# Loads of the FFN weights issued behind the DMA that turns the negated cosines

## The chip, the cores and the metric

The kernel runs on one core of a Trainium2 chip. The metric is the device time of one execution in microseconds (us). Every run also gives its span, from the first instruction to the last, which is some 1.8 us shorter than the time. Unless said otherwise, runs are fast (a run more than 1.5% above the fastest of its kernel is marked slow), and times in a profile count from the start of its span.

## The reference

A pre-LN block on x of 2048 x 512: a spectral filter, then an FFN with squared ReLU, both with residuals.

```python
X = rfft2(layernorm(x)) * (w_r + 1j * w_i)
h = x + irfft2(X)
r = relu(layernorm(h) @ w1 + b1)         # 512 -> 1792
out = h + (r * r) @ w2 + b2              # 1792 -> 512
```

## The kernel before

The two FFTs are matmuls against tables of sines and cosines that the kernel makes itself. Stage 4 (the first inverse step) needs tables in the other orientation, the tile EI, with four parts: sine, cosine, negated sine, negated cosine. Each is a DMA transpose ("turn") from SBUF to SBUF, issued on the queue of SyncE (SP), which issues all plain loads too. The part that the change touches, with the pieces of work that come after it in program order:

```python
def turned(dst, src):
    nc.sync.dma_start_transpose(out=dst, in_=...)

table_c(slice(1, 8))                                  # ScalarE: cosines
turned(EI[:, 1:8, 1, :], EF[:, 1, 1:8, :])            # the turn of the cosines
def cos_negs():                                       # runs at "cn.0" of ORDER
    nc.vector.tensor_scalar(Cn[:], EF[:, 1, 1:8, :], -1.0, None, ALU.mult)
    turned(EI[:, 1:8, 3, :], Cn[:])                   # EI<-Cn, the turn in question
# ... (first pieces of stage 2)
for k, (dst, src) in enumerate(((W1[:], ...), (W2[:], ...), (b1b[:], ...), (b2b[:], ...))):
    load = nc.sync.dma_start(dst, src)                # 1792 KB, 1792 KB, 3.5 KB, 128 KB
    ...
def to_sqrt():                                        # "sq.0"
    nc.gpsimd.tensor_copy(b1f[:], b1b[:])
    nc.scalar.activation(junk1[:], eps[:], ACT.Sqrt, bias=eps[:])   # loads the table of Sqrt
ORDER = """ gn.0 s3.0 ... xa.0 cn.0 ...               # s4.k: matmuls of stage 4, slice k
    ... t.4 x.7 t.3 sq.0 s4.5 s4.6 A.7 B.7 y.7 z.7 m.7 n.7 t.5 t.6 s4.7 v.7 t.7 """
```

"x" and "t" are copies out of PSUM, the memory that matmuls write to (t.k into the tile T2 that stage 5 reads), mostly on ScalarE; v.7 is VectorE's half of the last. Most slices of stage 4 use sums and differences M of their data ("alternating halves of Z and M"). Only slices 5 and 6 work on Z itself, and they alone read the fourth part of EI:

```python
NO_M = (5, 6)
if M is None:                                         # slices 5 and 6; the line L500 of the profile
    en = ei[:, 2 * P:4 * P]                           # negated sine and negated cosine
    mms = [(u, r, ei[:, P:3 * P]) for u in range(2)]
    mms += [(u, 1 - r, en if u == r else ei[:, 0:2 * P]) for u in range(2)]
    for k, (u, c, tb) in enumerate(mms):
        nc.tensor.matmul(o, lhsT=Z[:, u, c, e::2], rhs=tb, start=(k == 0), stop=(k == 3))
```

## Time and profile before

| what | value |
|---|---|
| time, three runs | 164.94 us median (164.76 to 164.95) |
| the execution that was profiled | 164.48 us, span 162.7 us |
| negated cosines ready / EI<-Cn issued / landed | 22.7 / 37.5 / 41.7 us |
| stage-4 matmuls that read it could start | 40.9 us |
| first use of W1, of b1, of b2 | 53.0, 53.7, 61.7 us |

The time and the profiled execution are not of the same run, and they differ by 0.46 us. How busy the DMA engines are is seen by stretches of time. The columns are: stretch and its length, busy time (and instructions) of TensorE, its weight loads, VectorE, ScalarE and GpSimd, TensorE's granted clock (as a share of full speed), mean busy share of the 16 DMA engines, GB/s.

```profile
30.00:35.00 5.00, 4.95 (x42) 3.91 (x41) 5.00 (x13) 4.44 (x5) 0.00 (x0) 1.00 1.05 379
38.50:41.70 3.20, 2.53 (x21) 1.93 (x20) 3.17 (x8) 2.62 (x4) 0.27 (x1) 1.00 0.88 102
41.70:45.50 3.80, 3.73 (x35) 3.34 (x35) 2.79 (x7) 3.29 (x5) 0.00 (x0) 1.00 0.00 0
```

The engines are full while W comes in, the last stretch before 41.7 holds the end of the loads of b1 and b2 and then the turn, in small pieces (1003 of 1091 packets are under 512 bytes) at about a quarter of the rate, and afterwards there is no traffic. TensorE has 0.67 us unused in the middle row.

### The profile page before, as it was taken

What the parts mean: (1) busy time and instruction counts of PE and PEld (TensorE: products, weight loads), DVE (VectorE), ACT (ScalarE), POOL (GpSimd) and SP (SyncE); (2) the same over time, 40 slices, a digit from 0 to 9 for tenths busy, and PEclk for the clock granted to TensorE, in tenths of its full rate; (3) what the DMA queues carried; (4) which work ended last, traced back from release to release, by engine and by line L of the source; (5) the groups of instructions that cost most, each with busy time, mean ns of one, the idle gap of its engine ahead of it and who ended that gap; (6) DMA issues with size and microseconds to landing.
All of it is one profiled execution on the core that took longest, in us unless ns stands there. A gap on an engine that the chain in (4) does not pass through costs nothing.

```text
span 162.7 us, 2708 instructions
## 1 busy us (share of the span) xinstructions
PE 149.7 (92%) x934; PEld 87.5 (54%) x947; DVE 124.8 (77%) x320; ACT 105.5 (65%) x203; POOL 36.7 (23%) x64
## 2 busy tenths in 40 slices
PE   3959899999887999999899999999999999999990
PEld 1537675877663874666345454434454444565470
DVE  6999899999847798699995588995379984377221
ACT  4989889898967780598552897731389760288000
POOL 7868840000000005025000235000052300052000
PEclk9999999999999999999999999999999999999999
DMA  5986299999100000200000100024300005210011
GB/s 157 344 263 127 64 189 220 395 358 123 25 0 0 4 0 2 66 5 0 0 32 32 36 0 0 2 65 103 94 0 2 0 0 129 65 36 0 4 61 34
DMA packets 16430, 12.34 MB, mean 76 GB/s; under 512 B 10784, under 2 KB 14880, under 8 KB 16416
## 3 DMA queue, kind: packets, MB, share of 16 engines
q1 hardware_dynamic: 16256, 11.25, 25.8%
q0 software_dynamic: 160, 0.92, 2.6%
q8 instruction: 7, 0.11, 0.3%
q14 instruction: 7, 0.06, 0.1%
HBM read 8.01 MB, written 2.10 MB: 62 GB/s over the span
## 4 chain that ended last, share of the span: by engine, by line
PE 62%; DVE 22%; ACT 5%; issue 3%; DMA 3%; POOL 3%; ACTq 0%; DVEq 0%; POOLq 0%
PE po L742 26%; PE ph L709 21%; DVE act L713 4%; DVE st L217 3%; DMA EI<-Cn 3%; PE p L500 2%; PE po L730 2%; ACT rl L712 2%; PE p L346 2%; PE p L606 1%; POOL rs L224 1%; DVE Z L463 1%; DVE mB L456 1%; DVE mA L456 1%; DVE hs L610 1%
## 5 line engine op out<-in xcount | busy, mean ns | idle before, releaser
L712 ACT ACTIVATE rl<-ph,b1f 128x384 bf16<-128x384 f32 (+2 forms) x70 | 41.2, 616 | 22.4 <-PE ph L709 20.7
L709 PE MATMUL ph<-UT,W 128*128 128x384 bf16 (+2 forms) x277 | 51.5, 336 | 0.8 <-DVE UT L820 0.6
L742 PE MATMUL po<-W,act 128*128 128x512 bf16 x204 | 46.8, 379 | 0.3
L716 POOL TENSOR_TENSOR hb<-hs,b2b 128x512 f32<-128x512 bf16 x16 | 18.6, 1166 | 88.6 <-DVE act L713 88.6
L713 DVE TENSOR_TENSOR act<-rl 128x384 bf16<-128x384 bf16 (+2 forms) x70 | 31.3, 483 | 9.3 <-ACT rl L712 9.1
L709 PEld LDWEIGHTS <-W 128*128 128x128 bf16 x280 | 26.9, 98 | 21.1 <-issue 1.3
L742 PEld LDWEIGHTS <-act 128*128 128x128 bf16 x210 | 20.3, 98 | 24.8 <-issue 1.7
L746 DVE TENSOR_TENSOR ot<-po,hb 128x512 bf16<-128x512 f32 x15 | 10.3, 688 | 12.5 <-PE po L742 11.1
L257 PE MATMUL p<-ones 128*128 128x512 bf16 x22 | 7.1, 461 | 2.9 <-POOL ones L153 2.8
L243 PE MATMUL p<-KFr,xs 128*128 128x256 bf16 x32 | 7.3, 272 | 2.2 <-DVE KFr L228 2.2
L610 DVE SCALAR_TENSOR_TENSOR hs<-p,xs 128x512 bf16<-128x512 f32 x14 | 9.1, 681 | 0.0
L585 ACT CAST V<-p 128x512 bf16<-128x512 f32 x14 | 8.1, 593 | 0.0
L217 DVE BATCH_NORM_STATS2 st<-xs 128x6 f32<-128x512 bf16 x12 | 7.9, 677 | 0.0
L508 ACT CAST T<-p 128x1024 bf16<-128x1024 f32 x7 | 7.2, 1032 | 0.5 <-PE p L500 0.5
L245 PE MATMUL p<-KFr,xs 128*128 128x256 bf16 x32 | 7.3, 272 | 0.0
L346 PE MATMUL p<-GF,Bt 128*128 128x256 bf16 x56 | 7.1, 273 | 0.0
L621 ACT ACTIVATE junk<-hs 128x512 bf16<-128x512 bf16 x6 | 3.8, 628 | 5.1 <-DVE hs L610 5.1
L463 DVE TENSOR_TENSOR Z<-mA,mB 128x512 bf16<-128x512 bf16 x16 | 6.3, 422 | 0.6 <-PE p L500 0.5
L257 PEld LDWEIGHTS <-ones 128*128 128x128 bf16 x32 | 3.4, 110 | 6.2 <-POOL ones L153 2.8
L346 PEld LDWEIGHTS <-Bt 128*128 128x128 bf16 x56 | 5.5, 98 | 1.3
L383 ACT CAST U<-p 128x1024 bf16<-128x1024 f32 x6 | 6.1, 1032 | 0.0
L636 ACT ACTIVATE sd<-mv,eps 128x1 f32<-128x1 f32 (+2 forms) x10 | 2.7, 294 | 5.1 <-DVE mv L625 5.0
(188 smaller groups left out, 226.3 us busy)
## 6 DMA issues: line engine op xcount, KB each, us to landing
W<-in_B_w_dram SPq DMA_DIRECT2D x2, 1792.0 KB, 10.0
out_dram<-ot SPq DMA_DIRECT2D x15, 128.0 KB, 1.8
xs<-in_A_x_dram SPq DMA_DIRECT2D x3, 512.0 KB, 6.5
WB<-in_A_w_r_dram SPq DMA_DIRECT2D x1, 578.2 KB, 6.5
WB<-in_A_w_i_dram SPq DMA_DIRECT2D x1, 578.2 KB, 7.6
xs<-in_A_x_dram SPq DMA_DIRECT2D x2, 256.0 KB, 3.1
b2b<-in_B_b_dram SPq DMA_DIRECT2D x1, 128.0 KB, 9.4
out_dram<-ot SPq DMA_DIRECT2D x2, 64.0 KB, 1.5
```

The source lines that it names most:

```text
L217: nc.vector.bn_stats(st[:], xs[:, g, :])
L257: nc.tensor.matmul(o, lhsT=ones[:, 0:P], rhs=ones[:], start=True, stop=True)
L346: nc.tensor.matmul(puv[:, :, e, :], lhsT=Bt[:, 2 * t + 1 - e, 2 * pr + q, :], rhs=GFv[:, t, :, e, :], start=(t == 0), stop=(t == 1))
L463: nc.vector.tensor_tensor(Zs[pr][:, :, h], mA[:, :, h], mB[:, :, 1 - h], ALU.add if h else ALU.subtract)
L585: nc.scalar.copy(V[:].rearrange("p e h c -> p (e h c)"), pe[:])
L610: nc.vector.scalar_tensor_tensor(hs[:, g, :], Ys.pop(g)[:], WSC, xs[:, g, :], ALU.mult, ALU.add)
L709: nc.tensor.matmul(ph[:, 0:n], lhsT=W1[:, d, bass.ts(f, P)], rhs=UT[:, d, 0:n], start=(d == 0), stop=(d == ND - 1))
L712: nc.scalar.activation(rl[:, 0:n], ph[:, 0:n], ACT.Relu, bias=b1f[:, f:f + 1], scale=1.0)
L713: sq = nc.vector.tensor_tensor(act[:, f, 0:n], rl[:, 0:n], rl[:, 0:n], ALU.mult)
L716: add = nc.gpsimd.tensor_tensor(hb[:, g, :], hs[:, g, :], b2b[:], ALU.add)
L742: nc.tensor.matmul(po[:], lhsT=act[:, f, bass.ts(i, P)], rhs=W2[:, f, :], start=(f == 0), stop=(f == NF - 1))
L746: nc.vector.tensor_tensor(ot[:], po[:], hb[:, g, :], ALU.add)
```

## The change

Its intent is to send the turn that is wanted at 40.9 us ahead of the loads that are wanted from 53 us on. The loads become a function called just after the turn has been issued; nothing else changes.

```diff
-    for k, (dst, src) in enumerate(((W1[:], ...), (W2[:], ...), (b1b[:], ...), (b2b[:], ...))):
-        load = nc.sync.dma_start(dst, src)
-        ...
+    def first_loads():
+        cos_negs()
+        loads()
+
+    def loads():
+        for k, (dst, src) in enumerate(((W1[:], ...), (W2[:], ...), (b1b[:], ...), (b2b[:], ...))):
+            load = nc.sync.dma_start(dst, src)
+            ...
-                  ... cn=lambda k: cos_negs())
+                  ... cn=lambda k: first_loads())
```

More of the change, by code (lines that the diff above doesn't have):

```diff
@@ L515 @@
     stage2_one(1, 1, nc.scalar.copy)
-    for k, (dst, src) in enumerate(((W1[:], B_w1.rearrange("(c p) f -> p c f", p=P)),
-                                    (W2[:], B_w2.rearrange("(i p) d -> p i d", p=P)),
-                                    (b1b[:], B_b1.rearrange("(i p) -> p i", p=P)),
-                                    (b2b[:], B_b2.unsqueeze(0).to_broadcast([P, D])))):
-        load = nc.sync.dma_start(dst, src)
-        if k == 0:
-            for ga in gathers:
-                after(load, ga, "the rows of W first")
+    def first_loads():
+        cos_negs()
+        loads()
+    def loads():
+        for k, (dst, src) in enumerate(((W1[:], B_w1.rearrange("(c p) f -> p c f", p=P)),
+                                        (W2[:], B_w2.rearrange("(i p) d -> p i d", p=P)),
+                                        (b1b[:], B_b1.rearrange("(i p) -> p i", p=P)),
+                                        (b2b[:], B_b2.unsqueeze(0).to_broadcast([P, D])))):
+            load = nc.sync.dma_start(dst, src)
+            if k == 0:
+                for ga in gathers:
+                    after(load, ga, "the rows of W first")
     def angle_tables(k):
@@ L539 @@
                   s4=lambda k: stage4(k, split=(k == 7)), t=t_copy, v=t_copy, gi=lambda k: angle_tables(0),
-                  gn=lambda k: angle_tables(1), sq=lambda k: to_sqrt(), cn=lambda k: cos_negs())
+                  gn=lambda k: angle_tables(1), sq=lambda k: to_sqrt(), cn=lambda k: first_loads())
     ORDER = """
```

## The prediction

> **What bounds the kernel now.** I read the page first: the chain that ended last, for the line that has to do with the change. Most of it is TensorE in the FFN (L742 and L709); one entry belongs to the moved DMA.
>
> ```profile
> PE 62%; DVE 22%; ACT 5%; issue 3%; DMA 3%; POOL 3%; ACTq 0%; DVEq 0%; POOLq 0%
> ```
>
> So the DMA that turns the negated cosines (EI<-Cn) lies on the path that sets the end. Next the same chain in order of time (start, duration, what), around that DMA:
>
> ```profile
> 37.48 4.24 DMA EI<-Cn
> 41.77 3.45 PE p L500 x30
> 45.24 0.70 ACT T L508
> 46.17 0.58 ACT T L508
> 46.79 0.61 PE p L770 x4
> ```
>
> The chain walks from the landing of the DMA (41.72) to the stage-4 matmuls of L500, to the two ScalarE copies into T, to the first matmuls of stage 5. The 4.24 us are not what the DMA costs, since all engines had other work until 40.87. What it costs is read from the waits between 40 and 48 us (in total, times, longest):
>
> ```profile
> PE p L500 <- DMA EI<-Cn: 0.7, 1, 0.7
> DVE Z L463 <- PE p L500: 0.5, 1, 0.5
> ACT T L508 <- PE p L500: 0.5, 1, 0.5
> ```
>
> One wait of TensorE for the landing, and two that follow from it: VectorE wants a Z buffer that the late matmuls still read, ScalarE wants their result. Why does the DMA start at 37.48? The rows of the tile Cn say that its input was ready 15 us sooner, at 22.2 + 0.46 = 22.7:
>
> ```profile
> L332 DVE TENSOR_SCALAR Cn<-EF x1: 456/456/456, 22.2 to 22.2; 128x896 bf16<-128x896 bf16 x1
> ```
>
> The timeline of the queue SP says what it stood behind (start, time the queue was held):
>
> ```profile
> 19.16 5.90 SPq L260 DMA_TRANSPOSE EI<-EF  x4
> 25.48 0.94 SPq L520 DMA_DIRECT2D W<-in_B_w_dram  x2
> 26.47 5.03 SPq L520 DMA_DIRECT2D b1b<-in_B_b_dram  x1
> 31.55 5.83 SPq L520 DMA_DIRECT2D b2b<-in_B_b_dram  x1
> 37.48 2.20 SPq L260 DMA_TRANSPOSE EI<-Cn  x1
> ```
>
> Four loads hold the queue from 25.48 to 37.38, and none is wanted soon: W is first read at 53.0 (rows of the tile W), b1 by the activations from 53.71, b2 by GpSimd from 61.7. Last, ScalarE's timeline from 40 to 47 us, with the idle time before an instruction in brackets:
>
> ```profile
> 40.32 1.01 ACT L432 CAST X<-p 128x1024 bf16<-128x1024 f32 x1 [0.58 <-ACT T L508]
> 41.23 1.02 ACT L508 CAST T<-p 128x1024 bf16<-128x1024 f32 x1
> 42.27 1.28 ACT L533 ACT_TABLE_LOAD   x1
> 43.56 0.29 ACT L533 ACTIVATE junk<-eps 128x1 f32<-128x1 f32 x1
> 43.76 0.99 ACT L508 CAST T<-p 128x1024 bf16<-128x1024 f32 x1
> 45.24 1.01 ACT L508 CAST T<-p 128x1024 bf16<-128x1024 f32 x1 [0.48 <-PE p L500]
> 46.15 0.59 ACT L508 CAST T<-p4a 128x512 bf16<-128x512 f32 x1
> ```
>
> This engine is occupied without a break from 40.32 to 44.76 whatever the DMA does; only its 0.48 us before 45.24 come from the late matmuls. That row decides the size of the gain.
>
> **What the Trainium skill says.** The page "DMA: Bandwidth & Descriptors", section "Queues, rings and completion order": descriptors of one issuing queue are consumed in ring order on each DMA engine. So a transfer issued behind 3.6 MB of loads also moves behind them. The trace agrees: EI<-Cn lands at 41.72, after b2b's 31.55 + 9.4 = 40.95. "Perfetto Trace Analysis", section "Summary: the profiler window per engine type", says that a queue's row shows the issue and not the movement of data; here 2.20 us against 4.24 to the landing. The first page's "Rules for kernel authors" says that a non-contiguous last dimension becomes one descriptor per element; b1b, 3.5 KB in 2-byte pieces, holds the queue 5.03 us where each 1.8 MB load of W takes some 0.45. "ScalarE: Activation LUTs", section "What ACT_TABLE_LOAD costs", has about 1283 ns for the table load; the row above has 1.28 us.
>
> **The change part by part.** No instruction is added or removed, and the order on TensorE, VectorE, ScalarE and GpSimd stays; the listing of both kernels shows only SP changed: EI<-Cn goes from behind the four loads to ahead of them.
>
> (a) EI<-Cn. It becomes ready to issue when the queue is done with the previous turns, 19.16 + 5.90 = 25.06, Cn being there since 22.7. The turn just before it, of the same 7 blocks, held the queue 1.25 us and landed after 3.1 us. Taking 3.1 to 4.2 us, EI<-Cn lands at about 28.5 to 29.5, some 11 us before its first reader at 40.87. The DMA wait disappears.
>
> (b) The loads. They start later by what the turn takes in the queue and in the engines, 1.3 to 2.2 us: W1 lands near 35 instead of 25.48 + 7.4 = 32.9, W2 near 40 instead of 38.5, b1b and b2b near 42 to 43 instead of 41. From 20 to 37 us the DMA engines are busy 100% of the time and after 41.7 there is no traffic, so the same bytes in another order should end at about the same time. The margin to 53.0 is over 9 us. Cost on the path: none.
>
> (c) TensorE. The two first matmuls of L500 run at 40.65 as before; the other 30 start at 40.87 instead of 41.77, which frees 0.90 us (0.73 of it shown as idle, the rest modelled tail). At 0.109 us each, the 14 left of slice 5 end at 42.4; slice 6 needs Z, ready at 41.76, and ends at 44.15. Slice 7 takes 0.87, to 45.0 instead of 45.9.
>
> (d) VectorE. Its Z of slice 7 started at 43.49 with 0.53 idle. It is now free at 42.9, after slice 5 has been read (42.6), so M ends at 44.45 instead of 45.05; slice 7 reads the second half of M at 44.15 + 0.44 = 44.6. No new wait.
>
> (e) ScalarE. Slice 5's copy starts at 43.76 as before, because table load and X copy precede it. Slice 6's, whose matmuls are now done at 44.3, starts as soon as ScalarE is free: 45.24 - 0.48 = 44.76 (or 43.76 + 0.91 = 44.67, by the spacing of 45.24 to 46.15). The last copy starts at 45.6 to 45.7 instead of 46.15, its matmuls being done at 45.1.
>
> (f) Stage 5 at L770 waits for that copy: 46.79 - 0.5 = 46.3. From there every link is an engine waiting for an engine, so the tail shifts as a block.
>
> Sum: of the 0.90 us freed on TensorE about 0.5 come through, since ScalarE, not the DMA, is then the last to arrive. 164.94 - 0.5 = 164.4 us; span 162.7 to about 162.2.
>
> **The rivals.** First, the whole 0.9 us comes through (164.0). For it: the X copy at 40.32 has 0.58 us idle ahead of it, put down to a copy that ended at 39.74, so its real cause is unknown; VectorE, TensorE, or a stall that has to do with the busy DMA engines then. If the reordering removes it, ScalarE starts its last run up to 0.4 earlier, and TensorE's 0.9 is the limit. Against: nothing in the wait names a DMA.
>
> Second, the gain is eaten earlier (164.8 to 165.2). The turn now runs at 25 to 29 beside turns and gathers, where stage 3 feeds the chain through ScalarE; copies of one shape took 1.05 to 1.08 between 36 and 39 us and 1.01 to 1.04 otherwise. Ten copies slower by 0.05 would cost half a microsecond. Against: in that stretch VectorE is the busier engine, and ScalarE has a few tenths spare.
>
> Third, the loads become the wait: W or the biases arrive after 53 us and FFN matmuls stall (166 or more). It would need a delay of over 9 us where I see 2. Very unlikely.
>
> Fourth, nothing moves because another wait takes the place of this one at 40.87 (164.9): slice 6 needs a PSUM buffer, but the copy that frees it ended at 39.74. Unlikely.
>
> **Range and chances.** The runs of before lie within 0.2 us, so the spread is that of the rivals: 163.9 if the first holds fully, about 165.0 if the second eats the gain. I take 163.9 to 165.0 for 8 in 10, with 164.4 as the prediction. A change of 2% would be 3.3 us, beyond what any wait in the profile allows: 1% faster, 98% within, 1% slower.
>
> **What would show it.** Right: in the SP timeline EI<-Cn near 25.1 and W behind it; no wait of L500 for EI<-Cn; L500 as one run of matmuls from about 40.65; no idle ahead of ScalarE's copy of slice 6; L770 near 46.3; the FFN's first matmul at about 52.5 instead of 53.0; b1b and b2b down before 44. The chain then enters L770 through ScalarE's copies and table load. Wrong: an idle of more than 0.3 us on ScalarE between 43.5 and 45.5 (step e), stage-4 matmuls starting later than 40.65 (second rival), or any matmul of L709 waiting for W (third).

## The result, and the profile after

| | before | after |
|---|---|---|
| median, 4 runs each | 164.85 us (164.28 to 164.95) | 163.85 us (163.84 to 163.86) |
| span of the profiled execution | 162.7 us | 162.1 us |
| its time | 164.48 us | 163.86 us |
| L500 reads its last operand from | 41.77 us | no wait |
| first matmul of stage 5 | 46.79 us | 46.22 us |
| first matmul of the FFN | 53.01 us | 52.44 us |

The ratio is 0.9946, with a 95% interval of 0.9923 to 0.9970, so the change is faster by 0.3 to 0.8%. A ratio is the mean time of one kernel's fast runs over that of the other's of the same rounds, so it is not quite the ratio of the medians. The class is "same" (within 2%), as forecast.

The queue SP of the changed kernel (start, time the queue was held):

```profile
25.07 1.25 SPq L260 DMA_TRANSPOSE EI<-Cn  x1
26.43 1.10 SPq L525 DMA_DIRECT2D W<-in_B_w_dram  x2
27.57 4.78 SPq L525 DMA_DIRECT2D b1b<-in_B_b_dram  x1
32.40 7.18 SPq L525 DMA_DIRECT2D b2b<-in_B_b_dram  x1
```

EI<-Cn is issued at 25.07 and lands 3.1 us later, at 28.2, 12.7 us before it is read. The loads come 1 us later than before: b1b lands at 27.57 + 14.3 = 41.9 and b2b at 32.40 + 9.9 = 42.3. TensorE's row for L500 is now one run of 32 matmuls:

```profile
40.66 3.66 PE L500 MATMUL p<-EI,Z 128*128 128x256 bf16 x32
```

The chain that ended last (start, us, what) no longer has a DMA in this stage, but ScalarE's copies and its table load:

```profile
40.33 1.01 ACT X L432
41.34 0.91 ACT T L508
42.27 1.28 ACT L539
43.57 0.30 ACT junk L539
43.87 1.40 ACT T L508 x2
45.58 0.59 ACT T L508
46.22 0.61 PE p L776 x4
```

Between the two profiles stage 5 begins 0.57 us sooner, the FFN 0.57 us sooner, and the span is 0.6 us shorter: what is gained at 46 us is carried unchanged to the end. But the medians differ by 1.0 us. Two questions follow: is ScalarE what caps the gain at 0.57 us, and where do the other 0.4 us come from? How close VectorE is behind ScalarE is seen in its half of the last copy, which ends at 45.45 + 0.69 = 46.14 us, against 45.58 + 0.59 = 46.17 for ScalarE's. The matmuls that read VectorE's half are the second pair, and start 0.22 us after the first:

```profile
45.45 0.69 DVE L508 CAST T<-p4b 128x512 bf16<-128x512 f32 x1 [0.81 <-PE p4b L483]
```

### The profile page after: what moved, and what is told of

Read it like the earlier page. It is cut to its first block, busy times and chain, and to the rows that moved or that the text cites. A ratio compares the mean times of both kernels' runs of the same rounds, so it can differ in the third digit from the quotient of the medians.

```text
span 162.1 us, 2722 instructions
## 1 busy us (share of the span) xinstructions
PE 151.3 (93%) x947; PEld 87.7 (54%) x947; DVE 124.7 (77%) x320; ACT 105.6 (65%) x203; POOL 36.9 (23%) x64
## 4 chain that ended last, share of the span: by engine, by line
PE 73%; DVE 13%; ACT 6%; issue 3%; POOL 3%; ACTq 0%; DVEq 0%; POOLq 0%
PE po L748 27%; PE ph L715 25%; PE p L346 4%; DVE act L719 3%; DVE st L217 3%; PE po L736 2%; ACT T L508 2%; PE p L612 2%; POOL rs L224 1%; ACT rl L718 1%; PE p L585 1%; DVE KFr L228 1%; PE p L672 1%; PE p L502 1%; PE p L503 1%
## 5 line engine op out<-in xcount | busy, mean ns | idle before, releaser
L718 ACT ACTIVATE rl<-ph,b1f 128x384 bf16<-128x384 f32 (+2 forms) x70 | 41.2, 615 | 22.4 <-PE ph L715 20.7
L748 PE MATMUL po<-W,act 128*128 128x512 bf16 x210 | 47.6, 379 | 0.0
L257 PE MATMUL p<-ones 128*128 128x512 bf16 x23 | 7.9, 499 | 2.8 <-POOL ones L153 2.8
```

Of the source, the lines that this page charges most:

```text
L257: nc.tensor.matmul(o, lhsT=ones[:, 0:P], rhs=ones[:], start=True, stop=True)
L718: nc.scalar.activation(rl[:, 0:n], ph[:, 0:n], ACT.Relu, bias=b1f[:, f:f + 1], scale=1.0)
L748: nc.tensor.matmul(po[:], lhsT=act[:, f, bass.ts(i, P)], rhs=W2[:, f, :], start=(f == 0), stop=(f == NF - 1))
```

## The experiments

My theory has two parts. The wait for the landing of EI<-Cn costs what it lasts, less what ScalarE's own work hides; and that landing moves from run to run, so the kernel before is longer in its median than in the execution that happened to be profiled. Rivals: the megabytes of W, not the order of the last small loads, delay the turn; TensorE or VectorE rather than ScalarE caps the gain; the traffic itself slows the engines. Eleven runs were made, all with correct results. They are of two chips (e5 to e8 on one, the others on the other), and the record doesn't say on which chip the first comparison ran, so times are best compared within one chip.

### e1: the kernel before again

No edit.

> The kernel before, unchanged, to see where its runs of 164.28 to 164.95 us differ, while the changed kernel repeats within 0.02 us. Theory (the wait for the landing of EI<-Cn is what varies): the runs spread over some 0.7 us again, ratio 1.0 within 0.3%, and in a profile whose span is longer than 162.7 us the idle of TensorE before L500 is longer than 0.73 us by as much. Rival (the spread comes from somewhere else): the idle stays at 0.7 us and a longer span shows in another place.

Measured: 164.72 us median of 6 (164.19 to 165.05). This profile came from a run of 165.05 us with a span of 163.2. Its wait, and TensorE's row behind it:

```profile
PE p L500 <- DMA EI<-Cn: 1.3, 1, 1.3
```

```profile
42.35 3.44 PE L500 MATMUL p<-EI,Z 128*128 128x256 bf16 x30 [1.31 <-DMA EI<-Cn]
```

The idle is 1.31 us where the first profile has 0.73, a difference of 0.58, and the matmuls go on 0.58 us later. The span is 0.5 us longer. The theory's forecast holds for these two: they are executions of one kernel and differ by the wait for this landing. It was issued at 37.65 (37.48 in the first profile) and took 4.7 us (4.2). Why the DMA takes longer in one run than in another is not shown.

### e2 and e3: the turn between the loads

```diff
# from the changed kernel; e2: k == 2 (behind W1 and W2), e3: k == 3 (behind b1b too)
 def cos_negs():
     nc.vector.tensor_scalar(Cn[:], EF[:, 1, 1:8, :], -1.0, None, ALU.mult)
-    turned(EI[:, 1:8, 3, :], Cn[:])
 # in the loop of loads()
+    if k == 2:
+        turned(EI[:, 1:8, 3, :], Cn[:])
     load = nc.sync.dma_start(dst, src)
```

> EI<-Cn issued behind W1 and W2 (3.58 MB) but ahead of b1b and b2b (0.13 MB). Theory (what counts is only whether it lands before about 41.3 us, and the last 0.13 MB decide that): W2 lands at about 38.5, the turn 2 to 2.5 us later, near 40.5 to 41; nearly the whole gain stays, 163.85 to 164.1 us, idle before L500 0 to 0.2 us. Rival (the megabytes of W are what delays it): as the kernel before, 164.8 us, idle 0.7 us.

> EI<-Cn issued behind W1, W2 and b1b (1792 pieces of 2 bytes), ahead of b2b. Theory: landing near 41, between those of e2 and of the kernel before; 163.9 to 164.5 us. Rival (the order against b2b is what counts, b1b costs nothing): as e2. Rival (b1b alone is the trouble): as the kernel before, 164.8 us.

Measured: e2 163.94 us (163.83 to 164.06), no wait at L500, the turn landing at 26.44 + 14.2 = 40.6. e3 164.02 us (163.97 to 164.67), the turn landing at 31.64 + 9.6 = 41.2, and a short wait:

```profile
41.29 3.43 PE L499 MATMUL p<-EI,Z 128*128 128x256 bf16 x30 [0.23 <-DMA EI<-Cn]
```

So W ahead of the turn (two loads of 1792 KB, 3.67 MB; the expectation counts 1000 bytes to a KB) costs nothing that a median shows: e2 stands beside 163.99 us for the changed kernel on the same chip (e11). The rival, that W alone makes the wait, falls. But W delays the landing most, from 28.2 to 40.6 us, and so uses up nearly all the slack. The two little loads, 0.13 MB together, then move it from 40.6 to 41.7 us, and that is the whole wait. How this 1.1 us divides between b1b and b2b is not shown, since each landing is of one profile and one kernel's landing moved by 0.6 us (e1). In e3 only two of six runs, 164.65 and 164.67, are as long as the kernel before: it stands at the edge. e2's margin is thin as well (0.2 us), the change's is 12.7 us.

The queue SP of e2 also corrects a reading of the prediction:

```profile
26.44 8.41 SPq L260 DMA_TRANSPOSE EI<-Cn  x1
34.90 0.58 SPq L526 DMA_DIRECT2D b1b<-in_B_b_dram  x1
35.53 4.19 SPq L526 DMA_DIRECT2D b2b<-in_B_b_dram  x1
```

And that of e3:

```profile
26.41 5.13 SPq L526 DMA_DIRECT2D b1b<-in_B_b_dram  x1
31.64 7.70 SPq L260 DMA_TRANSPOSE EI<-Cn  x1
39.39 0.58 SPq L526 DMA_DIRECT2D b2b<-in_B_b_dram  x1
```

I had put the 5.03 us in which b1b holds the queue down to its 2-byte pieces. Here b1b takes 0.58 us, and the turn, which takes 1.25 us ahead of the loads, takes 8.41. Whatever is issued next behind the 3.67 MB of W is held, small or not. A queue's row is thus no measure of its own DMA when a large one stands before it. That the queue waits for room among the pieces of W not yet moved is my inference; no run shows it.

### e4 and e10: a longer wait

```diff
# from the kernel before, behind the loop of loads and ahead of the turn; e10: 0:1 instead of 0:2
+    nc_extra = persist.tile([P, 2, F], BF16, name="extra")
+    nc.sync.dma_start(nc_extra[:], B_w1.rearrange("(c p) f -> p c f", p=P)[:, 0:2, :])
```

> The kernel before with one more load of 0.92 MB into a tile nobody reads, ahead of EI<-Cn. Theory (once the landing is later than about 41.3, each microsecond of it costs one): 0.92 MB at some 350 GB/s make the landing 2.6 us later, so 164.85 + 2.6 = 167.4 us, idle of TensorE before L500 about 3.3 us. Rival (part of the wait hides behind ScalarE and VectorE): less than 1.5 us longer.

> The kernel before with 0.46 MB more ahead of EI<-Cn, half of e4's. e4 waited 4.39 us, 3.66 more than before, and its span grew by 5.3, as TensorE's granted clock fell to 0.59 in the 3.6 us after the wait. Theory (the fall of the clock comes only with a long idle): wait about 2.5 us, granted clock stays 1.0, span 162.7 + 1.8 = 164.5, 166.4 us. Rival (the clock falls with any such idle, in proportion): clock under 0.9 after the wait, 167 us or more.

Measured: e4 168.43 to 171.61 us over four runs, two of them marked slow, the profiled one 169.84 with span 168.0. e10 166.72 to 168.16 us, median 167.45 (ratio 1.0179, 1.0129 to 1.0229: unclear at 2%), the profiled run 166.72 with span 164.9. Both expectations were too low. TensorE's rows behind the wait, e4 first and then e10:

```profile
45.42 5.10 PE L500 MATMUL p<-EI,Z 128*128 128x256 bf16 x30 [4.39 <-DMA EI<-Cn]
```

```profile
43.99 3.44 PE L500 MATMUL p<-EI,Z 128*128 128x256 bf16 x30 [2.85 <-DMA EI<-Cn]
```

The same 30 matmuls take 5.10 us in e4 and 3.44 us in e10 and in the kernel before. By stretches (columns as above, the clock is the third number from the end), e4 and then e10:

```profile
41.00:45.40 4.40, 0.03 (x1) 0.00 (x0) 1.96 (x4) 2.83 (x4) 0.02 (x1) 1.00 0.72 240
45.40:49.00 3.60, 3.58 (x20) 2.70 (x20) 0.93 (x3) 0.96 (x1) 0.00 (x0) 0.59 0.00 0
46.10:49.40 3.30, 3.30 (x18) 2.38 (x16) 1.33 (x4) 1.01 (x1) 0.00 (x0) 0.50 0.00 0
```

```profile
43.90:47.50 3.60, 3.50 (x33) 3.14 (x33) 1.52 (x4) 1.11 (x3) 0.00 (x0) 1.00 0.00 0
```

After 4.39 us without matmuls the granted clock was 0.59 for the next 3.6 us, as a mean: it was still 1.00 until 46.0, 0.50 from 46.1 to 49.4, and 1.00 again from 49.5. After 2.85 us it was 1.00. The Trainium skill, "TensorE: Matmul & The Clock Gate", "Part 1: The HAM clock gate", says that the clock falls to half after an idle window of about 3.4 us. The two traces agree, one on each side of that figure, and with the half; where between 2.85 and 4.39 us the limit lies, no run shows. For the profiled runs the account closes: e4 goes on at 45.42 instead of 41.77 (3.65 us later) and loses 5.10 - 3.44 = 1.66 us to the clock, 5.31 together; its span is 168.0 - 162.7 = 5.3 us longer. e10 goes on 2.22 us later, its span is 2.2 longer. So in these two runs each microsecond of wait costs one, until it is long enough for the clock; my "each costs one" failed for e4 by leaving the clock out, and the added load also delayed the landing by more than its bytes at 350 GB/s (3.65 instead of 2.6 us). The two last runs of e10 (spans 166.3 and 166.1, mean clock 0.99) look like a fall of the clock as well, and so does the slow run of the kernel before (167.54 us, clock 0.99), but they have no profile.

### e5 and e6: is it ScalarE that caps the gain?

```diff
# e5: the kernel before; e6: the changed kernel; in to_sqrt()
     nc.scalar.activation(junk1[:], eps[:], ACT.Sqrt, bias=eps[:])
+    nc.scalar.activation(junk1[:], eps[:], ACT.Sqrt, bias=eps[:])
```

> The kernel before with ScalarE's little square-root activation after the table load issued twice (0.3 us more on ScalarE, just ahead of its stage-4 copies). Theory (in the kernel before the late matmuls are the last to arrive, ScalarE waits 0.5 us for them): the 0.3 us vanish in that idle; from the restart of L500 after EI<-Cn to the first stage-5 matmul it stays 46.79 - 41.77 = 5.02 us, and the time stays in the range of before. Rival (ScalarE already bound there): 5.3 us, 0.3 us longer.

> The changed kernel with the same 0.3 us more on ScalarE. Theory (step e: with the wait gone ScalarE arrives last and caps the gain): stage 5 begins 0.3 us later than 46.22, at about 46.5, and the time is 163.85 + 0.3 = 164.15 us. Rival (TensorE or VectorE caps it): stage 5 still begins at 46.2, 163.85 us.

Measured: e5 164.80 us (164.56 to 165.16), ratio 1.0024 with an interval of 1.0001 to 1.0048; e6 164.14 us (164.12 to 164.15). By its time alone e5 is just longer, which would favour the rival, but runs of this kernel differ by more than 0.3 us with the landing, so the profile must decide. In e5 L500 goes on at 41.95 (idle 0.92) and stage 5 begins at

```profile
46.98 0.61 PE L771 MATMUL p<-GIa,T 128*128 128x256 bf16 x4 [0.50 <-ACT T L508]
```

which is 5.03 us after it, where the kernel before has 46.79 - 41.77 = 5.02: the 0.3 us on ScalarE left no trace. In e6 the same instruction, put into the changed kernel, shifts everything:

```profile
46.54 0.61 PE L777 MATMUL p<-GIa,T 128*128 128x256 bf16 x4 [0.93 <-ACT T L508]
```

Stage 5 is 0.32 us later than in the changed kernel, and the time 0.29 us longer than in the first comparison, 0.20 than that of e8, which does the same work at this place and ran on the chip of e6. Before the change ScalarE had room and the DMA was last; after it ScalarE is last. Together with e1, e3 and e10 this gives a simple rule for the start of stage 5 in these kernels: the later of 46.22 us (ScalarE) and 5.02 us after L500 goes on. e3 gives 41.29 + 5.02 = 46.31, and 46.31 us is measured; e10 gives 49.01, measured 49.02. So the first 0.3 us of the wait were always hidden: 46.22 - 5.02 = 41.20, against 40.66 + 0.22 = 40.88 for matmuls that don't wait.

### e7 and e9: less work on ScalarE

```diff
# e7: from the changed kernel; in ORDER t.6 becomes w.6
+    def t_halves(pr):
+        src = P4[pr][0][:].rearrange("p (l q g s) -> p l g q s", l=4, q=2, g=G)
+        for h, cp in ((0, nc.scalar.copy), (1, nc.vector.tensor_copy)):
+            cp(T2[:, 2 * h:2 * h + 2, :, 2 * pr:2 * pr + 2, :], src[:, 2 * h:2 * h + 2])
# e9, in addition: slice 6 into two PSUM tiles, and slice 7 one half after the other
-    P4[pr] = pts = [mm_tile("p4a"), mm_tile("p4b")] if split else [mm_tile("p4")] * 2
+    P4[pr] = pts = [mm_tile("p4a"), mm_tile("p4b")] if split or pr == 6 else [mm_tile("p4")] * 2
-            pt = pts[0]
+            pt = pts[e]
-            src = P4[pr][0][:].rearrange(...)           # in t_halves, now inside its loop
+            src = P4[pr][h][:].rearrange(...)
-            for u, tb in ((0, ei[:, P:3 * P]), (1, ei[:, 0:2 * P])):
-                for m in range(4):
+            for u, tb, ms in ((0, ei[:, P:3 * P], (0, 1)), (1, ei[:, 0:2 * P], (0, 1)),
+                              (0, ei[:, P:3 * P], (2, 3)), (1, ei[:, 0:2 * P], (2, 3))):
+                for m in ms:
```

> The changed kernel with the copy of slice 6 into T halved between ScalarE and VectorE, which is idle from 44.64 to 45.45. A try at a version that beats both. Theory (ScalarE caps the gain): its last copy starts at about 45.25 instead of 45.57, stage 5 at about 45.9 instead of 46.22, 163.85 - 0.3 = 163.55 us. Rival (something else caps it, or VectorE's half delays its own last copy): 163.85 us or more.

> As e7, but slice 6 goes into two PSUM tiles, so that VectorE's half no longer waits for ScalarE's (e7 lost 0.65 us there); slice 7's matmuls finish one half before the other. Theory (ScalarE's copies cap the changed kernel): VectorE's half runs at 44.65 to 45.3, its last copy ends near 46.1, stage 5 begins at about 45.85 and goes on without a gap; 163.85 - 0.3 = 163.55 us. Rival (another wait takes its place, such as the PSUM buffer of slice 5): 163.8 us or more.

Measured: e7 163.98 us (163.96 to 163.98), no gain. ScalarE's last copy did start at 45.21, but VectorE's new half waited for ScalarE's:

```profile
45.27 0.69 DVE L514 CAST T<-p 128x512 bf16<-128x512 f32 x1 [0.65 <-ACT T L514]
```

The trace names ScalarE's half of the same copy, which reads the same PSUM tile, as what it waited for. This puts VectorE's last copy 0.43 us later (45.88 instead of 45.45), and the second pair of stage-5 matmuls waits for that. With two tiles (e9) the wait is gone, so the shared PSUM tile was its cause:

```profile
44.57 0.68 DVE L515 CAST T<-p4b 128x512 bf16<-128x512 f32 x1
45.58 0.69 DVE L509 CAST T<-p4b 128x512 bf16<-128x512 f32 x1 [0.33 <-PE p4b L484]
```

Stage 5 begins at 45.81 us, and e9 takes 163.67 us (five of six runs 163.65 to 163.70, one 163.98), against 163.99 us for the changed kernel on the same chip (e11). It beats both kernels, by far less than 2%. Its gain was forecast as 0.3 us and is 0.32 by these medians, 0.18 against the 163.85 us of the first comparison, and 0.21 by the start of the FFN in the profiles (52.23 instead of 52.44). The first four matmuls of stage 5 now take 0.91 us instead of 0.61, still waiting for VectorE's last copy, so only half of the 0.41 us at 45.81 comes through. VectorE's last copy was only some 0.3 us from being the limit in the changed kernel (it ended at 46.14, and its matmuls began at 46.22 + 0.22 = 46.44), so a cut on ScalarE alone could bring no more than that, which is an estimate from these rows.

### e8: more bytes, but behind the turn

```diff
# from the changed kernel
     def loads():
+        nc.sync.dma_start(extra[:], B_w1.rearrange("(c p) f -> p c f", p=P)[:, 0:2, :])
```

> The changed kernel with the 0.92 MB load of e4 in the same queue, but behind EI<-Cn and ahead of W. Theory (bytes behind the turn cost nothing, since W is wanted only at 52.4): W, b1b and b2b land 2.6 us later, by 45, and the time stays 163.85 us. Rival (the loads themselves are near the path, or the traffic slows the engines): 164.2 us or more.

Measured: 163.94 us (163.94 to 164.01), span 162.1 us as for the changed kernel. b2b lands at 34.41 + 11.0 = 45.4. The 0.92 MB that cost e4 five microseconds ahead of the turn cost at most 0.1 behind it. Here the order decides, not the bytes.

### e11: the changed kernel again

No edit.

> The changed kernel, unchanged, beside e9 on one chip. Theory (its landing has 11 us to spare, so the spread of the DMA does not reach the time): all runs within 0.1 us of 163.85, while the runs of before in the same rounds spread over 0.5 us or more. Rival (the small spread was luck of four runs): a spread like that of before.

Measured: 163.99 us (163.88 to 164.26), ratio 0.9956 (0.9923 to 0.9988). The spread is 0.38 us, so my "within 0.1" failed, and the 0.02 us of the first four runs was in part luck; it is still less than that of the kernel before, whose runs on the same chip went from 164.24 to 166.05 (and one of 167.54, marked slow). The profiled run, 164.08 us, has no wait at L500, but stage 4's L500 starts at 40.83 instead of 40.66. The delay comes from the start of the program, where ScalarE's sums wait for the first rows of x, and GpSimd for those sums. The waits from 3 to 20 us, and GpSimd's row:

```profile
ACT junk L209 <- DMA xs<-in_A_x_dram: 1.2, 2, 1.0
```

```profile
13.32 0.33 POOL L223 TENSOR_SCALAR rs<-mv 128x4 f32<-128x4 f32 x1 [0.21 <-ACT junk L209]
```

In the first profile of the changed kernel ScalarE waited 0.3 us there and GpSimd not at all, starting at 13.15, 0.17 us sooner. So one exposed DMA is gone and another, at the start, is left; it is in the kernel before as well.

## Why the prediction was right or wrong

- The wait and its cause (step a): right. EI<-Cn was issued at 25.07 where 25.06 was forecast, landed at 28.2 (28.5 to 29.5 forecast), and nothing waits for it.
- The loads (step b): right. They were issued 1 us later instead of 1.3 to 2.2 and landed by 42.3. The prediction overlooked that in the kernel before the load of W1 waited 0.4 us for a gather into WB, a wait that is gone in the changed kernel: part of the turn fits into it. e8 shows that there was room for 3 us more.
- TensorE and VectorE (steps c and d): right but for 0.2 us. L500 starts at 40.66 and is one run, and no new wait arose on VectorE. But its Z of slice 7 starts at 43.08 (42.9 forecast), M ends at 44.64 (44.45), and slice 7's matmuls start at 44.36 (44.15). This cost nothing, as ScalarE came last.
- ScalarE caps the gain (step e): right, and shown by the pair e5 and e6. Of the two values I gave for its next copy, 44.76 by the idle time and 44.67 by the spacing of copies, the spacing was the better one, so that stage 5 begins at 46.22 instead of the 46.3 predicted. The gain in the profile is 0.57 us, not 0.5.
- The tail shifts as a block (step f): right; the FFN starts at 52.44 (52.5 forecast).
- The sum: the term mis-sized is "0.5 come through", as taken off 164.94 us. It was worked out from an execution that took 164.48 us, whose wait was 0.73 us, and subtracted from the median of others, whose wait was not looked at. From its own run the sum is 164.48 - 0.57 = 163.9, and 163.86 us was measured. e1's profile has the other kind of run: a wait of 1.31 us and 165.05 us, where by the rule above the change takes away 1.2. The median fell by 1.0 us, which fits runs with waits between these two, but they have no profile, so that is likely and not shown. It lies at 163.85, just under the range I gave, while the repeat (e11) gave 163.99 us against 164.71 us, 0.72 less. The range itself rested on the kernel before repeating within 0.2 us, by three runs; a fourth gave 164.28, and e1's six went from 164.19 to 165.05.
- The rivals: the first (0.9 us come through because ScalarE's idle ahead of its X copy vanishes) is refuted, since that idle is 0.58 us in both kernels; the median fell by about as much for another reason. The second, slower copies from 25 to 29 us, did not show: L500 starts at 40.66 as against 40.65. The third and fourth did not happen.
- The remark that b1b holds the queue because of its 2-byte pieces was wrong (e2).

## What to carry to other kernels

Within one queue, order DMAs by when their data is wanted, not by when they can be issued: here 0.13 MB of loads wanted 12 us later or more cost 0.6 to 1.2 us (by two profiles) by standing ahead of a turn whose slack 3.67 MB of other loads had used up. The wait for this DMA, near the path, differed between runs (0.73 and 1.31 us), so work out a gain from the time of the profiled execution itself and look at more than one profile. Before counting a removed wait in full, find which engine arrives next, and test it by adding a little work to that engine in both kernels.

## What the Trainium skill lacked or had wrong

- "Perfetto Trace Analysis", "Summary: the profiler window per engine type", says that a DMA's row on its queue is issue time, a wait for a lock included, and not data movement, but gives no figure for how this time grows with what stands ahead: the same turn held the queue for 1.25 us ahead of W and 8.41 us behind it (e2), and b1b for 0.58 to 5.13 us.
- "DMA: Bandwidth & Descriptors", "Latency and other measured facts", gives 261 GB/s for a DMA transpose. Here two turns of 7 x 128 x 128 bf16 values (229 KB) landed one after the other at 26.8 and 28.2 us (changed kernel), which is an estimate of 164 GB/s, and the profile has 141 GB/s of all traffic in these 1.4 us; the page has no figure for turns of this size.
- No page that I read says that a DMA's landing varies between executions of one kernel: EI<-Cn took 4.2 us in one and 4.7 us in another, and with its later issue the wait for it was 0.73 and 1.31 us.
